# Moving one row in twenty-eight of the last weight matrix to 64 partitions, in a one-core decode block

## The chip, the cores and the metric

One core of a Trainium2 chip runs the kernel. The metric is the device time of one execution in microseconds (us): 139.9 us, the median of three executions (139.68 to 140.05).

## What is computed

A decode step of four sequences, one token each, through one transformer block: attention over the last 2048 positions of a cache (32 query heads, 4 key and value heads of 128 elements), and a gated feed-forward layer, each behind a layer norm and with a residual. Everything is bf16 in memory.

```python
def _B_ref(x, w1, w3, w2):                     # D = 1024, F = 3584
    gate = jnp.einsum("bsd,df->bsf", x, w1)
    up = jnp.einsum("bsd,df->bsf", x, w3)
    h = _silu(gate) * up
    out = jnp.einsum("bsf,fd->bsd", h, w2)
    return out
x = A_x
h = x + _A_ref(_layernorm(x, axis=-1), A_k_cache, A_v_cache, A_wq, A_wo)
h2 = h + _B_ref(_layernorm(h, axis=-1), B_w1, B_w3, B_w2)
```

With four tokens, nearly all of the work is to bring 55.6 MB of caches and weights into the core once.

## The kernel before, in words

**The stream.** All large inputs pass through a ring of five slots (`NSLOT`, 32 KB for each of 128 partitions). The list `ring` (L107 to L115) gives the order: keys, wq, values, wo, w1, w3, w2. `fill()` (L120 to L135) hands out the next slot as soon as the slot's former tenant is used, and issues the tenant's transfers from SyncE's queue at L133. A tenant is one transfer of up to 4 MB, or two of 2 MB (keys, values, and wo with `wo_` at L101), or, for the last slot of w2, three: `W2B = [16, 8, 2, 2]` (L108) cuts the 28 rows that each partition has of w2 into one slot of 16 rows and one slot of 8, 2 and 2. A partition's rows are adjacent in memory, `"(p fc) n -> p fc n"` (L79), and one row is 2 KB. In every one of these transfers each partition gets one piece, so one transfer is 128 pieces for the 16 DMA engines of the core.

**The order of the work** is the program's own order (`manual_schedule`). On SyncE's queue the transfers stand in the ring's order, and each waits for its slot. After attention, the output projection (L434, weights wo) gives h1 (L444); the second layer norm runs on VectorE (`layernorm_T`). `up_projection` (L448 to L466) is called for w1 and then for w3: for each of eight chunks of D, 8 matmuls (L458) of 448 columns fill two PSUM tiles of 32-partition groups. Between the two, ScalarE and VectorE make silu of the gate: exp (L472), plus one (L473), reciprocal (L474), multiply (L476). After w3, VectorE multiplies (L480) and transposes (L225) to `hg_T`, which has 28 groups of 128 values of F. The last matrix product (L491) takes w2's rows in the order in which their transfers come, four matmuls of 256 columns to a row, accumulating in one PSUM tile. VectorE adds h1 (L501), and two queues write the result (L503, L504).

**The two small transfers at the ends** matter for reading the trace. The input x is loaded by a transfer of ScalarE's queue (L149) whose access pattern has an outer dimension of 4 at its source and 16 partitions at its destination. Each half of the result is written by a transfer with an outer dimension of 2 at its destination.

Of the kernel before, what the change touches and what calls it, by code (L numbers as in the profile page):

```python
# [10 lines left out]
P = 128  # L11
ACT = mybir.ActivationFunctionType
ALU = mybir.AluOpType
AX = mybir.AxisListType
BF16 = mybir.dt.bfloat16
FP32 = mybir.dt.float32
# [7 lines left out]
def kernel(  # L24
# [20 lines left out]
    nc = tc.nc  # L45

    B, _, D = A_x.shape
    Hkv, Sk, Dh = A_k_cache.shape[1], A_k_cache.shape[2], A_k_cache.shape[3]
    NQ = A_wq.shape[1]
    Hq = NQ // Dh  # L50
    REP = Hq // Hkv
    W = min(4096, max(256, Sk // 4))
    F = B_w1.shape[1]
    KC = D // P
    FC = F // P
    NK = W // P
    C = 4
    R = 32
    S = R // B
    DQ = D // C  # L60
    FQ = F // C
    FH = FQ // 2
    assert B == C and Hkv == C and B * Hq == P and Dh == P and REP * Hkv == R
    assert D == KC * P and F == FC * P and W == NK * P and NQ == Hq * Dh
    eps = 1e-5
    qscale = float(Dh) ** -0.5

# [3 lines left out]
    T = REP  # L71
# [4 lines left out]
    wo_v = A_wo.rearrange("(g p t) n -> p g (t n)", g=Hkv, t=T)  # L76
    w1_v = B_w1.rearrange("(p kc) f -> p kc f", kc=KC)
    w3_v = B_w3.rearrange("(p kc) f -> p kc f", kc=KC)
    w2_v = B_w2.rearrange("(p fc) n -> p fc n", fc=FC)  # L79

    const = ctx.enter_context(tc.tile_pool(name="const", bufs=1))
    act = ctx.enter_context(tc.tile_pool(name="act", bufs=1))
# [3 lines left out]
    ps = ctx.enter_context(tc.tile_pool(name="ps", bufs=1, space=bass.MemoryType.PSUM))  # L86
# [6 lines left out]
    def pair(parts):  # L93
        return [parts[0:2], parts[2:4]]
# [3 lines left out]
        for name, cache in (("k", A_k_cache), ("v", A_v_cache))  # L98
    )
    kT_ = pair([("kT", b, [JR, P], None) for b in range(B)])  # L100
    wo_ = pair([("wo", g, [1, T * D], wo_v[:, g : g + 1, :]) for g in range(Hkv)])  # L101

    def four_rows(name, view, n):
        return [[(name, i, [4, n], view[:, 4 * i : 4 * i + 4, :])] for i in range(KC // 4)]

    wq_ = four_rows("wq", wq_v, NQ)
    ring = k_ + wq_[:1] + kT_ + wq_[1:] + v_ + wo_ + four_rows("w1", w1_v, F) + four_rows("w3", w3_v, F)  # L107
    W2B = [16, 8, 2, 2]  # L108
    w2_ = []
    f0 = 0  # L110
    for i, n in enumerate(W2B):
        w2_.append(("w2", i, [n, D], w2_v[:, f0 : f0 + n, :]))
        f0 += n
    ring += [w2_[:1], w2_[1:]]
    views = {}  # L115
    taken = []
    used = set()
# [1 line left out]
    def fill():  # L119

        while len(taken) < len(ring):
            n = len(taken) - NSLOT
            if n >= 0 and not all((name, i) in used for name, i, _, _ in ring[n]):
                break
            parts = ring[len(taken)]
            slot = stream.tile([P, SLOT], BF16, tag="slot", name="s_" + parts[0][0])
            o = 0
            for name, i, shape, src in parts:
                dst = slot[:, o : o + int(np.prod(shape))]
                o += int(np.prod(shape))  # L130
                view = dst.rearrange("p (a b) -> p a b", a=shape[0])
                if src is not None:
                    nc.sync.dma_start(out=dst if name in ("k", "v") else view, in_=src)  # L133
                views[(name, i)] = view
            taken.append(slot)  # L135

    def get(name, i):
        return views[(name, i)]

    def done(name, i):  # L140
        used.add((name, i))
        fill()
# [5 lines left out]
    nc.vector.memset(x_nat[:], 0.0)  # L148
    nc.scalar.dma_start(out=x_nat[::S, :], in_=x_flat.rearrange("b (c n) -> c b n", c=C))  # L149
    fill()  # L150

    ident = const.tile([P, P], BF16)
# [8 lines left out]
        out=t32[:], in_=ident[:].rearrange("p (q h) -> p h q", q=C), axis=AX.X, op=ALU.add  # L161
# [4 lines left out]
    for q in range(C):  # L166
# [3 lines left out]
        out=negm[:], in_=t32[:].rearrange("p (g r) -> p g r", g=Hkv), axis=AX.X, op=ALU.add  # L170
    )
    nc.vector.tensor_scalar(
        out=negm[:], in0=negm[:], scalar1=-1.0, scalar2=-NEG, op0=ALU.add, op1=ALU.mult
# [3 lines left out]
        out=jmask[:, :, 0], in_=ident[:].rearrange("p (j h) -> p j h", j=JM), axis=AX.X, op=ALU.add  # L177
# [6 lines left out]
    for l in range(2):  # L184
        nc.gpsimd.tensor_copy(
            out=strip[:, l, B - 1 :].rearrange("p (c x) -> p c x", c=C)[:, :, : B * Hkv].rearrange(
                "p c (g b) -> p c g b", b=B
            )[:, :, :, 0],
            in_=t32[:].rearrange("p (g c l) -> p l c g", g=Hkv, c=C)[:, l],
        )  # L190

    def layernorm_T(h_T, tag):

# [29 lines left out]
    def transpose_quads(dst, src, n):  # L223

        nc.vector.transpose(  # L225
            out=dst.rearrange("p j r -> p (j r)"), in_=src.rearrange("p (q j) -> p j q", j=n)
        )
# [24 lines left out]
    for i in range(KC // 4):  # L252
        w = get("wq", i)
        for kk in range(4):
            kc = 4 * i + kk
            for hf in range(2):
                for c in range(C):
                    o = (2 * c + hf) * HALF * Dh
                    nc.tensor.matmul(  # L259
                        q_ps[hf][R * c : R * c + R],  # L260
                        lhsT=xn_T[:, kc, :],
                        rhs=w[:, kk, o : o + HALF * Dh],
                        start=(kc == 0),
                        stop=(kc == KC - 1),
                        tile_position=(0, R * c),
# [12 lines left out]
    for b in range(B):  # L278
        nc.vector.tensor_copy(  # L279
            out=Qm[:, b].rearrange("p (g y) -> p g y", y=QW)[:, :, :REP],  # L280
            in_=qT_ps[:, :, :, S * b].rearrange("p r g -> p g r"),
# [125 lines left out]
    for l in range(2):  # L407
        for b in range(B):
            nc.tensor.matmul(  # L409
                on_ps[:, l],  # L410
                lhsT=strip[:, l, B - 1 - b : B - 1 - b + P],
                rhs=om[:, b],
                start=(b == 0),
                stop=(b == B - 1),
# [8 lines left out]
        out=oP[:, :, :, ::S],  # L423
        in_=oX[:, :, : Hkv * B].rearrange("p t (g b) -> p g t b", b=B),
# [2 lines left out]

    y_ps = ps.tile([P, DQ], FP32, tag="kt0")
    for g in range(Hkv):
        w = get("wo", g)  # L430
        for t in range(T):
            for c in range(C):
                o = t * D + c * DQ
                nc.tensor.matmul(  # L434
                    y_ps[R * c : R * c + R, :],
                    lhsT=oP[:, g, t, :],
                    rhs=w[:, 0, o : o + DQ],
                    start=(g == 0 and t == 0),
                    stop=(g == Hkv - 1 and t == T - 1),
                    tile_position=(0, R * c),  # L440
                )
        done("wo", g)
    h1 = act.tile([P, DQ], FP32)
    nc.vector.tensor_tensor(out=h1[:], in0=y_ps[:], in1=x_nat[:], op=ALU.add)  # L444
    h_T = act.tile([P, KC, R], FP32)
# [1 line left out]
    hn_T = layernorm_T(h_T[:], "ln2")  # L447


    def up_projection(name, out_ps):  # L450
        for i in range(KC // 4):
            w = get(name, i)
            for kk in range(4):
                kc = 4 * i + kk
                for hf in range(2):
                    for c in range(C):
                        o = c * FQ + hf * FH
                        nc.tensor.matmul(  # L458
                            out_ps[hf][R * c : R * c + R],
                            lhsT=hn_T[:, kc, :],  # L460
                            rhs=w[:, kk, o : o + FH],
                            start=(kc == 0),
                            stop=(kc == KC - 1),
                            tile_position=(0, R * c),
                        )
            done(name, i)  # L466

    gu_ps = [ps.tile([P, FH], FP32, tag=f"sc{i}", name=f"gu_ps{i}") for i in range(4)]
    up_projection("w1", gu_ps[:2])
    eg = act.tile([P, 2, FH], FP32)  # L470
    for hf in range(2):
        nc.scalar.activation(out=eg[:, hf], in_=gu_ps[hf][:], func=ACT.Exp, scale=-1.0)  # L472
    nc.vector.tensor_scalar_add(out=eg[:], in0=eg[:], scalar1=1.0)  # L473
    nc.vector.reciprocal(out=eg[:], in_=eg[:])  # L474
    for hf in range(2):
        nc.vector.tensor_tensor(out=eg[:, hf], in0=gu_ps[hf][:], in1=eg[:, hf], op=ALU.mult)  # L476
    up_projection("w3", gu_ps[2:])
    hg = act.tile([P, 2, FH], BF16)
    for hf in range(2):
        nc.vector.tensor_tensor(out=hg[:, hf], in0=gu_ps[2 + hf][:], in1=eg[:, hf], op=ALU.mult)  # L480
    hg_T = act.tile([P, FC, R], BF16)
    transpose_quads(hg_T[:], hg[:].rearrange("p a f -> p (a f)"), FC)


    y2_ps = ps.tile([P, DQ], FP32, tag="kt1")
    fc = 0
    for i, n in enumerate(W2B):
        w = get("w2", i)
        for ff in range(n):
            for c in range(C):  # L490
                nc.tensor.matmul(  # L491
                    y2_ps[R * c : R * c + R, :],
                    lhsT=hg_T[:, fc, :],
                    rhs=w[:, ff, c * DQ : (c + 1) * DQ],
                    start=(fc == 0),
                    stop=(fc == FC - 1),
                    tile_position=(0, R * c),
                )
            fc += 1
    res = act.tile([P, DQ], BF16)  # L500
    nc.vector.tensor_tensor(out=res[:], in0=y2_ps[:], in1=h1[:], op=ALU.add)  # L501
    out_v = out_flat.rearrange("b (c n) -> c b n", c=C)
# [32 lines left out]
```

## Time and profile before

| what | value |
|---|---|
| median of three executions | 139.9 us |
| the profiled execution | 140.13 us, span in the profile 138.3 us |
| busy: TensorE matmuls, VectorE, ScalarE, GpSimd | 80.2, 52.9, 42.7, 4.2 us |
| moved by SyncE's queue (q1) | 55.58 MB, 94.4% of 16 engines' span |
| mean rate over the span | 403 GB/s |
| last weights landed (trace, from the span's start) | 134.26 us |

The profile's times run from the first instruction to the last. A DMA queue's share is the time that its packets took, as a share of the span of all 16 DMA engines. Beside the page, the trace records when a transfer's semaphore was raised: each DMA engine that took part raises it once, when its own share has landed, so a transfer on 16 engines leaves 16 times. The waiting instruction goes on at the last of them.

### The profile page before, as it was taken

How to read it: one execution, taken by the hardware profiler on the slowest of the kernel's cores; microseconds unless marked ns; L12 is line 12 of the kernel's file. 1: busy time of each engine (PE TensorE's matmuls, PEld its weight loads, DVE VectorE, ACT ScalarE, POOL GpSimd, SP SyncE). 2: the span in 40 equal slices, each digit the busy share in tenths (PEclk: the TensorE clock that was granted, in tenths of full speed). 3: DMA queues.
4: the chain of work that ended last, by engine and by line, in shares of the span. 5: the costliest groups of instructions: out<-in, count | busy, mean ns of one | idle time of the engine just before them, and what ended most of it. 6: DMA issues, size and time to landing. Idle time of an engine off the chain costs nothing.

```text
span 138.3 us, 2012 instructions
## 1 busy us (share of the span) xinstructions
PE 80.2 (58%) x866; PEld 47.5 (34%) x868; DVE 52.9 (38%) x97; ACT 42.7 (31%) x57; POOL 4.2 (3%) x18
## 2 busy tenths in 40 slices
PE   0029898921903889328918998659539901703780
PEld 0029887820301322014304434537324400202550
DVE  3036676520000235177087197540330298350001
ACT  3005988850000325998807900000040200000000
POOL 7400000000000000000000000000000000000000
PEclk9999999998555799975797799965865896555555
DMA  4999999999989999999999999999999999999930
GB/s 152 399 423 431 431 436 455 455 441 398 445 384 426 441 417 417 450 407 431 450 400 431 433 469 431 394 448 448 419 398 448 456 411 430 445 407 398 406 148 2
DMA packets 3217, 55.72 MB, mean 403 GB/s; under 512 B 360, under 2 KB 392, under 8 KB 648
## 3 DMA queue, kind: packets, MB, share of 16 engines
q1 hardware_dynamic: 3178, 55.58, 94.4%
q8 instruction: 7, 0.11, 0.3%
q10 hardware_dynamic: 30, 0.01, 0.0%
q14 instruction: 2, 0.02, 0.0%
HBM read 55.58 MB, written 0.01 MB: 402 GB/s over the span
## 4 chain that ended last, share of the span: by engine, by line
DMA 49%; PE 27%; DVE 13%; ACT 4%; SPq 3%; issue 2%; DVEq 0%
DMA s_wq<-in_A_wq_dram 29%; DMA s_w<-in_B_w_dram 20%; PE o_ps L369 10%; PE y_ps L434 5%; ACT P L334 4%; PE sc_ps L294 3%; DVE PT L346 3%; SPq L133 3%; PE gu_ps L458 2%; PE q_ps L259 2%; DVE om L386 2%; DVE od L378 2%; PE on_ps L409 1%; PE tot_ps L355 1%; PE nm_ps L323 1%
## 5 line engine op out<-in xcount | busy, mean ns | idle before, releaser
L334 ACT ACTIVATE P<-sc_ps,bias 128x512 bf16<-128x512 f32 x16 | 19.7, 1417 | 9.6 <-DVE bias L331 9.6
L241 PE MATMUL kt_ps<-ident,s_k 128*128 128x128 bf16 x256 | 17.3, 228 | 1.3 <-ACT s_kT L245 1.0
L369 PE MATMUL o_ps<-s_v,PT 128*128 128x512 bf16 x62 | 17.5, 439 | 0.3 <-issue 0.2
L241 PEld LDWEIGHTS <-s_k 128*128 128x128 bf16 x256 | 16.3, 103 | 2.3 <-issue 1.7
L245 ACT COPY s_kT<-kt_ps 128x1024 bf16<-128x1024 bf16 x16 | 15.7, 1012 | 2.5 <-PE kt_ps L241 2.5
L458 PE MATMUL gu_ps<-s_w,n_T 128*32 128x448 bf16 x128 | 10.7, 513 | 8.8 <-DMA s_w<-in_B_w_dram 6.8
L259 PE MATMUL q_ps<-s_wq,n_T 128*32 128x512 bf16 x64 | 7.0, 615 | 11.8 <-DMA s_wq<-in_A_wq_dram 11.8
L243 DVE COPY s_kT<-kt_ps 128x1024 bf16<-128x1024 bf16 x16 | 11.1, 693 | 5.8 <-PE kt_ps L241 5.8
L491 PE MATMUL y_ps<-s_w,hg_T 128*32 128x256 bf16 x112 | 6.6, 418 | 8.0 <-DMA s_w<-in_B_w_dram 8.0
L369 PEld LDWEIGHTS <-PT 128*128 128x128 bf16 x64 | 7.2, 117 | 9.2 <-issue 4.4
L346 DVE STREAM_TRANSPOSE PT<-P 128x2048 bf16<-128x2048 bf16 x4 | 9.2, 2303 | 2.7 <-ACT P L334 2.7
L208 ACT ACTIVATE rstd<-rstd,eps_t 128x4 f32<-128x4 f32 x2 | 0.6, 297 | 29.5 <-DVE rstd L207 29.5
L458 PEld LDWEIGHTS <-n_T 128*32 128x32 bf16 x128 | 4.7, 131 | 14.1 <-issue 11.6
L294 PE MATMUL sc_ps<-s_kT,Qm 128*32 128x512 bf16 x64 | 8.5, 603 | 0.4 <-DVE Qm L279 0.4
L491 PEld LDWEIGHTS <-hg_T 128*32 128x32 bf16 x112 | 4.9, 142 | 10.0 <-issue 5.9
L259 PEld LDWEIGHTS <-n_T 128*32 128x32 bf16 x64 | 2.7, 137 | 15.6 <-issue 15.5
L269 DVE CAST q_sb<-q_ps 128x512 bf16<-128x512 f32 x1 | 0.7, 692 | 18.3 <-PE q_ps L259 18.3
L198 PE MATMUL sums_ps<-both,ones_f 128*128 128x64 f32 x4 | 1.1, 373 | 11.2 <-DVE both L196 11.2
L434 PE MATMUL y_ps<-s_wo,oP 128*32 128x256 bf16 x128 | 6.5, 397 | 1.7 <-DVE oP L422 1.7
L378 DVE SCALAR_TENSOR_TENSOR od<-o_ps,rinv,jmask 128x512 f32<-128x512 f32 x4 | 3.0, 751 | 8.4 <-PE o_ps L369 8.3
L270 ACT CAST q_sb<-q_ps 128x512 bf16<-128x512 f32 x1 | 0.6, 585 | 17.8 <-PE q_ps L259 17.8
L310 PE MATMUL mx_ps<-ident_f,rmax 128*1 128x128 f32 x8 | 1.7, 302 | 7.4 <-DVE rmax L308 7.4
(68 smaller groups left out, 64.7 us busy)
## 6 DMA issues: line engine op xcount, KB each, us to landing
s_w<-in_B_w_dram SPq DMA_DIRECT2D x4, 3584.0 KB, 21.2
s_k<-in_A_k_cache_dram SPq DMA_DIRECT2D x4, 2048.0 KB, 16.1
s_wq<-in_A_wq_dram SPq DMA_DIRECT2D x2, 4096.0 KB, 35.3
s_v<-in_A_v_cache_dram SPq DMA_DIRECT2D x4, 2048.0 KB, 25.1
s_wo<-in_A_wo_dram SPq DMA_DIRECT2D x4, 2048.0 KB, 25.5
s_w<-in_B_w_dram SPq DMA_DIRECT2D x1, 4096.0 KB, 28.0
s_w<-in_B_w_dram SPq DMA_DIRECT2D x1, 2048.0 KB, 25.7
s_w<-in_B_w_dram SPq DMA_DIRECT2D x2, 512.0 KB, 27.0
```

What stands on the lines that cost most here:

```text
L241: nc.tensor.transpose(out=kt_ps[:, jj], in_=k[:, jb * JB + jj, :], identity=ident[:])
L243: nc.vector.tensor_copy(out=kT[:, jb * JB : (jb + 1) * JB], in_=kt_ps[:])
L245: nc.scalar.copy(out=kT[:, jb * JB : (jb + 1) * JB], in_=kt_ps[:])
L259: nc.tensor.matmul(q_ps[hf][R * c : R * c + R], lhsT=xn_T[:, kc, :], rhs=w[:, kk, o : o + HALF * Dh], start=(kc == 0), stop=(kc == KC - 1) ...
L294: nc.tensor.matmul(sc_ps[b][R * q : R * q + R], lhsT=Qm[:, b, g * R : (g + 1) * R], rhs=v[:, g, q], start=(g == 0), stop=(g == Hkv - 1), t ...
L334: nc.scalar.activation(out=P4[:, :, :, g], in_=sc_ps[b][:].rearrange("p (j i) -> p j i", i=L5), func=ACT.Exp, bias=bias[:, g : g + 1], sca ...
L346: nc.vector.transpose(out=PT[:].rearrange("p j h -> p (j h)"), in_=stage.pop(("P4", b))[:].rearrange("p j i g -> p (j i g)"),)
L369: nc.tensor.matmul(o_ps[:], lhsT=PT[:, i * JM : (i + 1) * JM, :].rearrange("p j h -> p (j h)"), rhs=v[:, i * JM : (i + 1) * JM, :], start= ...
L378: nc.vector.scalar_tensor_tensor(out=od[:], in0=o_ps[:], scalar=rinv[:, 0:1], in1=jmask[:].to_broadcast([P, JM, Dh]), op0=ALU.mult, op1=AL ...
L434: nc.tensor.matmul(y_ps[R * c : R * c + R, :], lhsT=oP[:, g, t, :], rhs=w[:, 0, o : o + DQ], start=(g == 0 and t == 0), stop=(g == Hkv - 1 ...
L458: nc.tensor.matmul(out_ps[hf][R * c : R * c + R], lhsT=hn_T[:, kc, :], rhs=w[:, kk, o : o + FH], start=(kc == 0), stop=(kc == KC - 1), til ...
L491: nc.tensor.matmul(y2_ps[R * c : R * c + R, :], lhsT=hg_T[:, fc, :], rhs=w[:, ff, c * DQ : (c + 1) * DQ], start=(fc == 0), stop=(fc == FC ...
```

## The change

F = 3584 is 28 x 128. Before, every partition had 28 rows of w2. After, every partition has 27 (the first 3456 rows), and the remaining 128 rows go to the first 64 partitions, two for each. These two rows come in two transfers of 32 partitions (128 KB each), ahead of the slot's other three, and their source has an outer dimension of eight. The slot's first large transfer shrinks from 8 rows to 7.

The columns of w1 and w3 are divided accordingly: 3456 into halves of 432 columns for each of four groups, and 128 into two groups of 64 columns, which a third, small PSUM tile holds (tags kt2 and kt0). Each of the eight chunks of D so has two more matmuls, and exp, multiply and the last multiply have a third, small instruction each. A second, small transpose gives `hx_T`, and the last product has eight more matmuls (64 rows deep), which follow w2's first 16 rows; in place of the 28th row's four. Apart from this, the four transfers of wo become two of 4 MB in the same two slots. GpSimd clears a corner of `eg` once, early.

```diff
-    FC = F // P
+    FC = F // P - 1
+    FM = FC * P
+    XP = P // 2
+    XR = 2
...
-    FQ = F // C
+    FQ = FM // C
     FH = FQ // 2
+    FX = 32 * XR
...
-    w2_v = B_w2.rearrange("(p fc) n -> p fc n", fc=FC)
+    w2_v = B_w2[:FM].rearrange("(p fc) n -> p fc n", fc=FC)
+    w2x_v = B_w2[FM:].rearrange("(c i e y) n -> c e i (y n)", c=XP // R, i=4, e=8)
...
-    wo_ = pair([("wo", g, [1, T * D], wo_v[:, g : g + 1, :]) for g in range(Hkv)])
+    wo_ = [[("wo", i, [2, T * D], wo_v[:, 2 * i : 2 * i + 2, :])] for i in range(Hkv // 2)]
...
-    W2B = [16, 8, 2, 2]
+    W2B = [16, 7, 2, 2]
...
-    ring += [w2_[:1], w2_[1:]]
+    ring += [w2_[:1], [("w2x", 0, [XR, D], w2x_v)] + w2_[1:]]
...
-                if src is not None:
+                if name == "w2x":
+                    for c in range(XP // R):
+                        nc.sync.dma_start(out=dst[R * c : R * c + R], in_=src[c])
+                elif src is not None:
...
+    eg = act.tile([P, FQ + FX], FP32)
+    nc.gpsimd.memset(eg[XP:, FQ:], 0.0)
...
+                for c in range(XP // R):
+                    nc.tensor.matmul(
+                        out_ps[2][R * c : R * c + R],
+                        lhsT=hn_T[:, kc, :],
+                        rhs=w[:, kk, FM + c * FX : FM + (c + 1) * FX],
...
+    hx_T = act.tile([XP, XR, R], BF16)
+    nc.vector.transpose(
+        out=hx_T[:].rearrange("p y r -> p (y r)"),
+        in_=hg[:XP, FQ:].rearrange("p (i e y) -> p y e i", i=4, e=8),
+    )
...
+            down(hg_T[:, fc, :], w[:, ff], fc == 0, fc == FC - 1)
             fc += 1
+        if i == 0:
+            for y in range(XR):
+                down(hx_T[:, y, :], get("w2x", 0)[:XP, y], False, False)
```

`down` is the former four matmuls of a row in a function.

More of the change, by code (lines that the diff above doesn't have):

```diff
@@ L60 @@
     DQ = D // C
-    FQ = F // C
+    FQ = FM // C
     FH = FQ // 2
+    FX = 32 * XR
     assert B == C and Hkv == C and B * Hq == P and Dh == P and REP * Hkv == R
-    assert D == KC * P and F == FC * P and W == NK * P and NQ == Hq * Dh
+    assert D == KC * P and F == FM + XP * XR and W == NK * P and NQ == Hq * Dh
     eps = 1e-5
@@ L429 @@
     for g in range(Hkv):
-        w = get("wo", g)
+        w = get("wo", g // 2)
         for t in range(T):
@@ L436 @@
                     lhsT=oP[:, g, t, :],
-                    rhs=w[:, 0, o : o + DQ],
+                    rhs=w[:, g % 2, o : o + DQ],
                     start=(g == 0 and t == 0),
@@ L441 @@
                 )
-        done("wo", g)
+        if g % 2 == 1:
+            done("wo", g // 2)
     h1 = act.tile([P, DQ], FP32)
@@ L465, in up_projection @@
                         )
-            done(name, i)
[L468 to L472, printed above, removed]
+                for c in range(XP // R):
[3 more added lines that the diff above has]
+                        rhs=w[:, kk, FM + c * FX : FM + (c + 1) * FX],
+                        start=(kc == 0),
+                        stop=(kc == KC - 1),
+                        tile_position=(0, R * c),
+                    )
@@ new lines, in up_projection, with parts @@
+            done(name, i)
+    gate_ps, up_ps = (
+        [
+            ps.tile([P, n], FP32, tag=tag, name=f"{name}_{tag}")
+            for n, tag in zip((FH, FH, FX), tags)
+        ]
+        for name, tags in (("gate", ("sc0", "sc1", "kt2")), ("up", ("sc2", "sc3", "kt0")))
+    )
+    def parts(t, three):
+        yield t[:, :FH], three[0][:]
+        yield t[:, FH:FQ], three[1][:]
+        yield t[:XP, FQ:], three[2][:XP]
+    up_projection("w1", gate_ps)
+    for e, g in parts(eg, gate_ps):
+        nc.scalar.activation(out=e, in_=g, func=ACT.Exp, scale=-1.0)
@@ L473 @@
     nc.vector.tensor_scalar_add(out=eg[:], in0=eg[:], scalar1=1.0)
     nc.vector.reciprocal(out=eg[:], in_=eg[:])
[L475 to L480, printed above, removed]
-    hg_T = act.tile([P, FC, R], BF16)
-    transpose_quads(hg_T[:], hg[:].rearrange("p a f -> p (a f)"), FC)
@@ L485 @@
-    y2_ps = ps.tile([P, DQ], FP32, tag="kt1")
+    for e, g in parts(eg, gate_ps):
+        nc.vector.tensor_tensor(out=e, in0=g, in1=e, op=ALU.mult)
+    up_projection("w3", up_ps)
+    hg = act.tile([P, FQ + FX], BF16)
+    for (h, u), (e, _) in zip(parts(hg, up_ps), parts(eg, up_ps)):
+        nc.vector.tensor_tensor(out=h, in0=u, in1=e, op=ALU.mult)
+    hg_T = act.tile([P, FC, R], BF16)
+    transpose_quads(hg_T[:], hg[:, :FQ], FC)
+    hx_T = act.tile([XP, XR, R], BF16)
+    nc.vector.transpose(
+        out=hx_T[:].rearrange("p y r -> p (y r)"),
+        in_=hg[:XP, FQ:].rearrange("p (i e y) -> p y e i", i=4, e=8),
+    )
@@ L486, with down @@
+    y2_ps = ps.tile([P, DQ], FP32, tag="kt1")
+    def down(lhsT, rows, start, stop):
+        for c in range(C):
+            nc.tensor.matmul(
+                y2_ps[R * c : R * c + R, :],
+                lhsT=lhsT,
+                rhs=rows[:, c * DQ : (c + 1) * DQ],
+                start=start,
+                stop=stop,
+                tile_position=(0, R * c),
+            )
     fc = 0
@@ L489 @@
         for ff in range(n):
[L490 to L498, printed above, removed]
+            down(hg_T[:, fc, :], w[:, ff], fc == 0, fc == FC - 1)
             fc += 1
+        if i == 0:
+            for y in range(XR):
+                down(hx_T[:, y, :], get("w2x", 0)[:XP, y], False, False)
     res = act.tile([P, DQ], BF16)
```

## The prediction

> **What bounds the kernel now.** I read the DMA slices of the page first, then the end of the chain of waits, then the queues, and last the semaphore times of single DMA engines.
>
> ```profile
> DMA  4999999999989999999999999999999999999930
> GB/s 152 399 423 431 431 436 455 455 441 398 445 384 426 441 417 417 450 407 431 450 400 431 433 469 431 394 448 448 419 398 448 456 411 430 445 407 398 406 148 2
> ```
>
> The DMA engines are never idle between their first bytes and about 134 us. Compute stages come and go under this line without denting it.
>
> ```profile
> 106.04 0.33 SPq L133
> 106.37 0.05 issue
> 106.42 0.43 SPq L133
> 106.84 0.05 issue
> 106.89 27.36 DMA s_w<-in_B_w_dram
> 134.26 0.04 issue
> 134.30 0.64 PE y_ps L491 x8
> 134.97 0.42 DVE res L501
> ```
>
> The columns are start, duration and what. The last transfer is issued at 106.89 and lands at 134.26: it stands in a queue that is 27 us deep. What follows is a fixed tail, 138.3 - 134.26 = 4.0 us in the span. So the time is the landing of the last piece plus a constant, and the question is when each of the 16 engines is through with its bytes. The 16 semaphore times of the last transfer (2 rows for each partition, 32 KB for each engine), divided into two halves that the next paragraph tells apart:
>
> ```
> 132.24 132.34 132.38 132.40 132.44 132.46 132.46 133.06
> 132.75 133.52 134.04 134.14 134.15 134.17 134.17 134.26
> ```
>
> All engines have had the same number of bytes, yet they end 2.02 us apart, and everybody waits for the last. Where the lag comes from is told by comparing transfers. At the second key transfer the 16 engines already form two halves, eight at 12.71 to 12.87 and eight at 12.98 to 13.23. After that single engines jump back: at the fourth key transfer fifteen end by 23.01 and one at 24.30, so 1.3 us late.
>
> ```profile
> q8 instruction: 7, 0.11, 0.3%
> q14 instruction: 2, 0.02, 0.0%
> ```
>
> The packets of q8 are 16 KB each and start at 20.53, 29.70, 52.31, 87.44, 100.18, 112.94 and 133.48 us; after each of the first six, one more engine of the late half is about 1.3 us behind. That they are instruction code of TensorE fits its counts: it had started 295, 519, 730, 981, 1260, 1457 and 1724 instructions by then, steps of 197 to 279. The two of q14 (8 KB; 69.91 and 77.69 us) cost one engine of the late half 0.8 us and one of the early half 0.65. Followed from transfer to transfer, that gives the two rows above: seven undisturbed early engines, one early engine disturbed (133.06), one undisturbed late engine (132.75), one with the 8 KB loss (133.52) and the six with the 16 KB loss, which set the time.
>
> **Does the change move bytes off these engines?** The number of engines that a transfer uses is seen at the small ones: x, with an outer dimension of 4, raised its semaphore from four engines, and each half of the result, with an outer dimension of 2, from two. So an outer dimension of eight should use eight. Which eight: x's four packets of 5.59 to 5.71 us delay the engines that began a key packet at 4.971, 5.030, 5.044 and 5.058 us, and the eight early engines are those that began at 4.971 to 5.058, the late half at 5.163 to 5.477. The four that a small transfer takes all lie in the early half; I take it that the eight do, too. The Trainium skill (DMA: Bandwidth & Descriptors, Queues, rings and completion order) says that the lowest-numbered engines are used, as many as divide the outer dimensions, which agrees with the four and the two seen here.
>
> **The sum.** Every engine loses one row of eight partitions, 16 KB. The 8-row transfer (128 KB for each engine) landed last at 126.83 to 131.73, 4.90 us, so one row is 4.90 / 8 = 0.61 us. The eight engines of the two new transfers get 2 x 16 KB in 4 KB pieces; the last two transfers have the same pieces, and 32 KB took 134.26 - 132.97 = 1.29 on the last engine, 132.24 - 130.97 = 1.27 on the first. I take 1.27. So the early half ends 1.27 - 0.61 = 0.66 later and the late half 0.61 earlier. The six go to 133.43 to 133.65, the seven early ones to 132.90 to 133.12, the disturbed early engine to 133.72. The last is now 133.72: a gain of 134.26 - 133.72 = 0.54 us. The profiled execution goes from 140.13 to 139.59, and the median, 0.23 below it, to 139.36, which I write as 139.4.
>
> **What the rest of the change costs: nothing, under cover.** SyncE issues two transfers more at 106.04 (0.33 to 0.43 each by the rows above), so its last issue moves from 107.3 to some 108.2; the first bytes of that slot move at about 126, so 18 us cover it. The two wo issues that go away were 30 us ahead of need (landed 83.1, first used 92.3), and each pair shares a slot, so no slot comes free earlier or later.
>
> ```profile
> 109.62 0.63 DVE L473 TENSOR_SCALAR eg<-eg 128x896 f32<-128x896 f32 x1 [6.85 <-ACT eg L472]
> 110.28 5.75 DVE L474 RECIPROCAL eg<-eg 128x896 f32<-128x896 f32 x1
> 116.14 1.16 DVE L476 TENSOR_TENSOR eg<-gu_ps,eg 128x448 f32<-128x448 f32 x2
> 120.02 1.16 DVE L480 TENSOR_TENSOR hg<-gu_ps,eg 128x448 bf16<-128x448 f32 x2 [2.72 <-PE gu_ps L458]
> 121.21 1.70 DVE L225 STREAM_TRANSPOSE hg_T<-hg 128x896 bf16<-128x896 bf16 x1
> ```
>
> VectorE's rows grow from 896 to 928 columns: the reciprocal by 5.75 x 32/896 = 0.2. The small multiplies have no row of their own; they lie between 0.17 (the smallest operations of L204 to L211) and 0.58 (half of L476), and I take 0.25 by the 128x32 rows of 0.19 to 0.30. Of the small transpose the nearest row is the 128x256 one with 0.63. The gate so ends under 1.2 us later than 117.3, but is needed at 120.0 only, when w3's matmuls end. Those are 40 where 32 took 3.18, at most 0.8 more; multiplies and transposes are at most 1.2 more; `hg_T` is ready by 124.9 where it was at 122.9, and w2's first rows land at 126.8. Cover of 1.9 us; if that were gone, some 0.9 us more would hide, because TensorE is otherwise through with all earlier rows 0.9 us before the last piece lands (next).
>
> ```profile
> 126.88 3.61 PE L491 MATMUL y_ps<-s_w,hg_T 128*32 128x256 bf16 x64 [6.53 <-DMA s_w<-in_B_w_dram]
> 131.77 2.33 PE L491 MATMUL y_ps<-s_w,hg_T 128*32 128x256 bf16 x40 [1.28 <-DMA s_w<-in_B_w_dram]
> 134.30 0.62 PE L491 MATMUL y_ps<-s_w,hg_T 128*32 128x256 bf16 x8 [0.20 <-DMA s_w<-in_B_w_dram]
> ```
>
> TensorE's eight new matmuls, 8 x 0.056 = 0.45, end at 130.95; the 7-row piece lands at about 131.1, its 28 matmuls (40 took 2.33) end by 132.8, and the last eight wait for the landing at 133.72 as before. The tail is unchanged.
>
> **Rules against it.** The trace shows one engine 2.02 us behind another with equal bytes. The Trainium skill (same page, Rules for kernel authors) says to put a multiple of 16 outermost, so that all engines share, and not to split transfers by partition halves; by it, with equal engines, the added 0.66 would be pure loss. It counts engines and not their lag, so I go by the trace. The skill (Runtime: NRT & Kernel Launch, Instruction fetch mechanics) also calls the cost of a fetched block of 256 instructions mostly hidden; for the engine that fetches it this trace has 1.3 us.
>
> **The rivals.**
>
> *The seventh code fetch comes early.* The change adds 64 TensorE instructions before w2. The fetch that started at 133.48, behind the data, will start 72 instructions or so earlier in the program, which is between 130 and 133 us, with weights still to move. On the undisturbed late engine it costs nothing that shows (132.14 + 1.3 = 133.44). On the engine with the 8 KB loss it gives 132.91 + 1.3 = 134.21, on an early one up to 133.12 + 1.3 = 134.42: no change within 0.16, so 139.85 to 140.1. Its cost lies between 0.61 (its own bytes) and 1.3. For it: six fetches hit six different engines of the late half, and two are left. Against: it may start when these are done. 0.17.
>
> *Slower: that fetch meets an engine that was already hit.* From 133.65, 1.3 more is 134.95, a loss of 0.69: 140.6. It decides if the fetch starts before about 133 and the engines come round again before the two are used. Nothing before shows a second hit. 0.10.
>
> *The new transfers spread over 16 engines*, two partitions each. Then every engine has its old bytes, and the time is 139.9. The four and two seen speak against. 0.08. *They fall on the late half*: 134.26 + 0.66 = 134.92, so 140.6. x's engines speak against. 0.05.
>
> **How the numbers follow.** Forecast 0.60, from 139.1 (no early engine disturbed and the full 0.61, less a spread of 0.2) to 139.6. A measurement of this kernel can tell 0.3% (0.42 us) from no change, and the gain of 0.54 is barely over it: of the 0.60 I give 0.46 to faster and 0.14 to the same. The same in all is 0.14 + 0.17 + 0.08 = 0.39, slower 0.10 + 0.05 = 0.15. The range runs from 139.1 to 140.1 and leaves the two slower cases out.
>
> **What would show it.** Right: eight landings for each of the two new transfers, all of early engines; the last transfer's 16 times within about 1.0 us, the last at 133.6 to 133.8. Wrong: a seventh packet of q8 before 133 with an engine alone behind the others; or a wait of the last matmuls for anything but the DMA.

## The result, and the profile after

The changed kernel takes 140.21 us (median of 11, 140.07 to 140.40) against 139.97 us (median of 11, 139.57 to 140.11): a ratio of 1.0021, 95% interval 1.0012 to 1.0029. So it is slower by 0.2%, some 0.24 to 0.29 us, where a gain of 0.54 us had been forecast. The profiled execution took 140.18 us, with a span of 138.4 us.

The DMA slices of the changed kernel:

```profile
DMA  4999999999989999999999999999999999999930
GB/s 152 418 417 450 426 412 450 455 450 436 436 374 417 445 421 417 440 426 412 450 419 417 438 465 406 427 456 423 403 439 456 414 419 470 407 389 423 398 129 2
```

As before, the DMA engines are full to the end, at the same rate. The end of its chain of waits (start, duration, what):

```profile
106.04 0.83 SPq L141
106.87 0.06 issue
106.92 0.72 SPq L141
107.65 0.04 issue
107.69 0.43 SPq L143
108.12 0.04 issue
108.16 0.43 SPq L143
108.59 0.04 issue
108.64 25.80 DMA s_w2x<-in_B_w_dram
134.43 0.04 issue
134.47 0.64 PE y_ps L529 x7
135.12 0.02 issue
135.14 0.42 DVE res L548
```

The shape is the same: the last transfer's landing, then a fixed tail. The landing is at 134.43, where it was at 134.26. The two new issues (L141) cost SyncE 0.83 and 0.72 us, more than the 0.33 to 0.43 of the other issues, and delay nothing: the transfer waits 25.80 us in its queue. TensorE's last product:

```profile
126.64 3.61 PE L529 MATMUL y_ps<-s_w,hg_T 128*32 128x256 bf16 x64 [6.46 <-DMA s_w<-in_B_w_dram]
130.18 0.61 PE L529 MATMUL y_ps<-s_w2x,hx_T 64*32 64x256 bf16 x8
131.97 2.11 PE L529 MATMUL y_ps<-s_w2x,hg_T 128*32 128x256 bf16 x36 [1.18 <-DMA s_w2x<-in_B_w_dram]
134.47 0.62 PE L529 MATMUL y_ps<-s_w2x,hg_T 128*32 128x256 bf16 x8 [0.40 <-DMA s_w2x<-in_B_w_dram]
```

In the brackets stands the idle time and what ended it: before each group after the eight new matmuls TensorE waits for the DMA and nothing else. So the loss must lie in when single DMA engines end. The semaphore times of the second new transfer and of the last transfer of w2:

```
126.04 126.05 126.06 126.09 126.15 126.80 127.05 127.63
131.75 131.76 132.00 132.86 132.86 132.87 132.97 133.25 133.27 133.28 133.36 133.37 133.60 133.85 134.42 134.43
```

The new transfer did land from eight engines. But they are not eight early ones: five are together, two are behind by 0.7 and 1.0 us (as engines with an 8 KB code fetch were before), and one by 1.5 us, like an engine with a 16 KB code fetch. It can be followed through the next transfers, 131.93, 133.18, 134.42: it is one of the two engines that the kernel waits for, and the other (134.43) is taken up below. The engines that got nothing are through by 133.37.

### The profile page after: what moved, and what is told of

The parts are those of the page before. It is cut to its first block, busy times and chain, and to the rows that moved or that the text cites. A ratio compares the mean times of both kernels' runs of the same rounds, so it can differ in the third digit from the quotient of the medians.

```text
span 138.4 us, 2092 instructions
## 1 busy us (share of the span) xinstructions
PE 80.8 (58%) x904; PEld 49.7 (36%) x904; DVE 53.3 (39%) x100; ACT 42.8 (31%) x58; POOL 4.4 (3%) x19
## 4 chain that ended last, share of the span: by engine, by line
DMA 47%; PE 28%; DVE 13%; SPq 4%; ACT 4%; issue 2%; DVEq 0%
DMA s_wq<-in_A_wq_dram 29%; DMA s_w2x<-in_B_w_dram 19%; PE o_ps L382 10%; PE y_ps L447 5%; ACT P L347 4%; PE sc_ps L307 3%; DVE PT L359 3%; SPq L143 3%; PE gate_sc L472 2%; PE q_ps L272 2%; DVE om L399 2%; DVE od L391 2%; SPq L141 1%; PE on_ps L422 1%; PE tot_ps L368 1%
## 5 line engine op out<-in xcount | busy, mean ns | idle before, releaser
L472 PEld LDWEIGHTS <-n_T 128*32 128x32 bf16 x128 | 5.6, 128 | 11.0 <-issue 7.8
L472 PE MATMUL up_sc<-s_w,n_T 128*32 128x432 bf16 x64 | 5.1, 453 | 6.6 <-DMA s_w<-in_B_w_dram 6.6
L272 PEld LDWEIGHTS <-n_T 128*32 128x32 bf16 x64 | 2.6, 137 | 15.6 <-issue 15.4
L529 PE MATMUL y_ps<-s_w,hg_T 128*32 128x256 bf16 x64 | 3.6, 419 | 6.5 <-DMA s_w<-in_B_w_dram 6.5
L472 PE MATMUL gate_sc<-s_w,n_T 128*32 128x432 bf16 x64 | 6.0, 546 | 1.9 <-DVE n_T L231 1.9
```

What stands on the lines that cost most here:

```text
L272: nc.tensor.matmul(q_ps[hf][R * c : R * c + R], lhsT=xn_T[:, kc, :], rhs=w[:, kk, o : o + HALF * Dh], start=(kc == 0), stop=(kc == KC - 1) ...
L472: nc.tensor.matmul(out_ps[hf][R * c : R * c + R], lhsT=hn_T[:, kc, :], rhs=w[:, kk, o : o + FH], start=(kc == 0), stop=(kc == KC - 1), til ...
L529: nc.tensor.matmul(y2_ps[R * c : R * c + R, :], lhsT=lhsT, rhs=rows[:, c * DQ : (c + 1) * DQ], start=start, stop=stop, tile_position=(0, R ...
```

## The experiments

**Who are the eight?** Two kernels, before and after, with five tiny transfers behind the last weights, of outer dimension 2, 4, 6, 8 and 12.

```diff
+            if len(taken) == len(ring):
+                for n, k in enumerate((2, 4, 6, 8, 12)):
+                    m = 256 + 32 * n
+                    nc.sync.dma_start(out=slot[:k, 14000 + 400 * n : 14000 + 400 * n + m], in_=B_w2[:k, :m])
```

> The kernel before with five tiny transfers (outer dimension 2, 4, 6, 8 and 12; 0.5 to 0.8 KB for each engine) at the end of SyncE's queue, behind the last weights. Each raises its semaphore from so many engines, each time behind that engine's own weights, so the nested sets tell which engines are late. Prediction's theory: the set of eight lies in the early half, all under 133.2 us, and all engines hit by a 16 KB code fetch are outside of it. Rival (the after trace hints at it): at least one of the eight is an engine hit by a 16 KB fetch, so one of the eight lands at about 133.7 to 134.2.

One execution: 140.09 us. The semaphore times of the last weights, and below them those of the tiny transfers with outer dimension 2, 4, 6 and 8:

```
132.36 132.37 132.38 132.40 132.46 132.53 132.54 132.72 133.38 133.48 133.86 134.01 134.08 134.10 134.15 134.19
k=2: 132.72 133.55
k=4: 132.63 132.90 133.66 133.72
k=6: 132.56 132.81 133.07 133.84 133.90 134.06
k=8: 132.58 132.59 132.74 132.98 133.25 134.01 134.06 134.26
```

As many landings as the outer dimension, each time. The sets are nested, and each further tiny transfer on an engine lands 0.16 to 0.20 us later (133.55, 133.72, 133.90 on one), so the new members can be told. Call an engine tight that no code fetch has put back, and 8 KB or 16 KB loss what a fetch of that size costs its engine. The first two engines are a tight one and one with an 8 KB loss, the next two the same, the third pair a tight one and one at 134.06, which has the full 16 KB loss, the fourth pair two tight ones. So the rival expectation holds: the eight hold one of the six engines with a 16 KB loss, and both engines with the smaller loss; the other five of the six lie outside.

> The changed kernel with the same five tiny transfers behind the last weights. Theory T (one engine among the eight of the new transfers had a 16 KB code fetch, and 0.66 us more on it sets the end): of the eight, one or two land at 134.3 to 134.5, the other six at 132.8 to 133.9; the eight others end by 133.4 except for none. Rival U (the seventh code fetch, now earlier, alone sets the end): the engine that is last is one that no earlier fetch had hit, and only it is beyond 134.

One execution: 140.44 us. The tiny transfer of outer dimension 6 ended at 134.69 on its last engine, the one of 4 at 134.30 and of 2 at 134.08: again the engine that comes in with the third pair is last. The last weights landed at 133.91, 134.12 and 134.50, the five engines with a 16 KB loss that lie outside at 133.49 to 133.71. Here one engine alone sets the end, as theory T has it. The other engines were later than it had them: 134.12 among the eight, where it allowed 133.9, and 133.71 outside, where it allowed 133.4. The size fits: in the probe of before this engine had its weights at 133.86 (one step of 0.20 before 134.06), and the forecast's own 0.66 more gives 134.52, against 134.50 here.

**Transfers or instructions?** Four kernels. The instructions of the change with the old transfers of w2 (the matmuls on the new rows read others):

```diff
-    w2_v = B_w2[:FM].rearrange("(p fc) n -> p fc n", fc=FC)
+    w2_v = B_w2.rearrange("(p fc) n -> p fc n", fc=FC + 1)
...
+        n += i == 1
...
-    ring += [w2_[:1], [("w2x", 0, [XR, D], w2x_v)] + w2_[1:]]
+    ring += [w2_[:1], w2_[1:]]
...
-                down(hx_T[:, y, :], get("w2x", 0)[:XP, y], False, False)
+                down(hx_T[:, y, :], w[:XP, y], False, False)
```

> The changed kernel's instructions with the transfers of w2 as before (28 rows for every partition in pieces of 16, 8, 2 and 2; no new transfers). The eight matmuls that would read the two new rows read two rows of the first piece again, so that part of the last product is computed from other rows of w2 than the reference has. The merged wo stays. Theory T (the 0.66 us more on eight engines, one of which had a 16 KB code fetch, is the cost): the last landing goes back by 0.2 to 0.35 us and the time to that of before (140.0, within 0.15). Rivals U and V (the earlier code fetch, the added instructions, the merged wo): it stays 0.2 to 0.3 us above before.

This kernel (m1): 139.93 us against 139.93, ratio 0.9996 (0.9984 to 1.0007). The cost is gone, though all added instructions on TensorE, VectorE and ScalarE and the merged wo are still there. This also shows that these cost nothing that can be measured. (The two added issues are gone too, with their transfers.)

The reverse, the old instructions with the new transfers:

```diff
+    w2_v = B_w2[: 27 * P].rearrange("(p fc) n -> p fc n", fc=27)
+    w2x_v = B_w2[27 * P :].rearrange("(c i e y) n -> c e i (y n)", c=2, i=4, e=8)
...
-    W2B = [16, 8, 2, 2]
+    W2B = [16, 7, 2, 2]
...
+    ring += [w2_[:1], [("w2x", 0, [2, D], w2x_v)] + w2_[1:]]
```

> The kernel before, its instructions kept, with the changed kernel's transfers of w2 alone (27 rows, and the two transfers on 64 partitions with outer dimension eight). The 28th row of the last product is read from 64 partitions of the new transfers, half as deep, so that row's part of the output is computed from half of the values. Theory T: slower by 0.2 to 0.3 us, as the change; one engine of the eight lands last, alone, near 134.5. Rivals U and V: no difference from before (within 0.1).

This kernel (m2): 140.44 against 139.93, 1.0032 (1.0022 to 1.0043). The new transfers alone, with their two issues, make the loss. The last transfer's end is 133.68, 134.01 and, alone, 134.71; the fetch that the old code makes late started at 133.74 here, too late for it. The loss, some 0.45 to 0.51 us, is larger than theory T had it (0.2 to 0.3) and than that of the change. The profile shows why it can be: here the late engine among the eight was the last of its six when w2's first rows had landed (126.65 of 126.46 to 126.65; it is the one at 127.29 after the first new transfer), so nothing of the 0.66 us was hidden, and in the changed kernel it was the first of its six (126.38 of 126.38 to 126.60).

The old transfers with the added matmuls of the up projections alone (32 matmuls of 64 columns each, into PSUM tiles that nobody reads):

```diff
+                for c in range(2):
+                    nc.tensor.matmul(
+                        more[R * c : R * c + R],
+                        lhsT=hn_T[:, kc, :],
+                        rhs=w[:, kk, 64 * c : 64 * c + 64],
```

> The kernel before with the 32 additional matmuls of 64 columns in the two up projections, into PSUM tiles that nobody reads; transfers as before. Theory T: the seventh code fetch starts earlier than 133.48, on an engine that has time (132.3 + 1.3 = 133.6), so no change, 139.97 within 0.15. Rival U: the fetch hits an engine that is already late, or the added instructions cost by themselves: 140.2 or more.

This kernel (d1): 140.13 against 140.03, 1.0001 (0.9992 to 1.0010). The seventh code fetch did move, from 133.48 to 131.97, and met an engine that had time: nothing is at 134 but the engines that were there before. In the changed kernel it starts at 132.24, and the engine at 134.43 beside the one at 134.42 is probably its doing (one of the five tight ones is missing in the last row). If so, the fetch alone would have set the same end in that execution. The loss does not need it, since the probe of after and the kernel with the new transfers alone have one engine alone at the end, at 134.50 and 134.71.

And twice the dose:

```diff
-    FC = F // P - 1
+    FC = F // P - 2
...
-    XR = 2
+    XR = 4
...
-    W2B = [16, 7, 2, 2]
+    W2B = [16, 6, 2, 2]
```

> The changed kernel with 26 rows for every partition and four more, in place of two, for the first 64 (8 KB pieces), so that the same eight engines get twice the extra. Theory T: 0.6 to 0.7 us more on the engine that is last: 140.8 to 141.0, the last landing at 135.0 to 135.2, with all eight others through by 133. Rivals U and V: as the change, 140.2 within 0.2, because the number of instructions hardly differs.

140.91 (four executions) against 139.93: 1.0065 (1.0048 to 1.0082), within the bounds of theory T. The last landing is at 135.06, 0.63 after that of the change, within its bounds too. Of the eight engines outside, four end by 131.35 and four at 133.40 to 133.65, where theory T had them through by 133; the eight loaded ones end at 132.61 to 135.06.

**Is it eight engines at all that matters?** The new transfers with an outer dimension of 32, so that all 16 engines take part:

```diff
-    w2x_v = B_w2[FM:].rearrange("(c i e y) n -> c e i (y n)", c=XP // R, i=4, e=8)
+    w2x_v = B_w2[FM:].rearrange("(c p y) n -> c p (y n)", c=XP // R, p=R)
...
-        in_=hg[:XP, FQ:].rearrange("p (i e y) -> p y e i", i=4, e=8),
+        in_=hg[:XP, FQ:].rearrange("p (q y) -> p y q", y=XR),
```

> The changed kernel with the two new transfers spread over 16 engines (32 pieces, one for each partition, outer dimension 32 in place of eight, rows given to partitions in plain order); all instructions, sizes and issues stay. Theory T (bytes on eight engines): every engine has its old bytes, the last landing goes back to about 134.1 to 134.3 and the time to that of before, 139.97 within 0.15. Rival V (what the change costs is in the added issues or instructions): it stays at 140.2. Rival U (the earlier code fetch): it stays at 140.1 to 140.3 if the fetch meets a late engine, 139.9 to 140.0 if it meets an early one.

This kernel (s1): 142.07 (four executions) against 140.03, 1.0145 (1.0124 to 1.0165). None of the theories had that; equal bytes should have brought the old time back. Its DMA slices:

```profile
DMA  4999999999999999999999999999999999999940
GB/s 149 412 415 438 429 433 470 391 433 447 447 415 396 438 433 429 405 443 433 436 401 440 453 424 420 457 416 432 453 408 408 440 455 447 401 295 232 399 169 2
```

The engines stay busy, but two slices, around 123 to 130 us, move 295 and 232 GB/s in place of some 400. There the two new transfers pass, and with them the transfer ahead of them, whose last rows came at 128.36 in place of 126.6. So I tried the same two transfers, on 16 engines too, to partitions that lie spread over all 128 (the matmuls read other rows):

```diff
-                        nc.sync.dma_start(out=dst[R * c : R * c + R], in_=src[c])
+                        nc.sync.dma_start(out=dst[2 * c :: 4], in_=src[c])
```

> As the spread over 16 engines that came out at 142.1, but the two new transfers write partitions 0, 4, 8, ... 124 and 2, 6, ... 126 in place of 0 to 31 and 32 to 63; the eight matmuls read rows of the first piece in their place, so that part of the last product is computed from other rows. Theory W (in the slow spread, engines wrote to partitions that other engines were writing too, and 256 KB went to the side of SBUF that serves 64 partitions): evenly over the partitions, the time falls to 140.0 to 140.7. Rival X (a transfer with 32 pieces of 4 KB on 16 engines is slow by itself): it stays at 142.0.

This kernel (q1): 140.13 against 139.93, 1.0012 (1.0001 to 1.0024). Its slices at the same place:

```profile
GB/s 142 390 437 441 427 427 465 455 422 427 427 389 432 432 408 441 432 408 450 427 405 450 420 479 407 411 432 473 407 403 440 473 403 439 446 390 405 395 171 2
```

The dip is gone (390 and 405), and each of the two transfers passes in some 0.31 us on every engine (124.91, 125.22, 125.54 on the first; 124.88, 125.61, 126.23 in the slow spread). So it is not the small pieces that are slow but where they go. The Trainium skill (SBUF — State Buffer, Door 1: The DMA port swizzle) says that a partition's number decides which of 16 ports its bytes come in by, and that partitions 0 to 63 reach eight of them. The two runs agree with that, with 2 us between them. Eight engines into the same 64 partitions, as in the change, are not slow: 16 KB take an engine 0.63 us there (125.41 to 126.04), close to the 0.61 us of 16 KB in the 8-row transfer. So it is the 16 engines and the 64 partitions together; which engines get in each other's way, and why it makes as much as 2 us, no run shows.

**Is it code that makes an engine late?** The kernel before, with the tiny transfers and 128 more small matmuls while TensorE waits for wq:

```diff
+        for _ in range(64):
+            nc.tensor.matmul(extra_ps[:R], lhsT=xn_T[:, 0, :], rhs=ident[:, :64], start=True, stop=True)
         w = get("wq", i)
```

> The kernel before, with the five tiny transfers at the end of the queue, and with 128 additional small matmuls (64 columns, with a weight load each, into PSUM that nobody reads) while TensorE waits for wq, so that 256 more instructions are fetched. If a code fetch is what puts a DMA engine back by 1.3 us: eight packets of 16 KB in q8, seven of them before 130 us, and seven engines in place of six some 1.4 to 1.9 us behind the tight ones at the last transfer, the last landing within 0.15 of before (134.2) where the added fetch meets a fresh engine, and 1.3 us later (135.5) where it meets one a second time. If the lag has another cause (a property of those engines, contention), six engines lag as before.

This kernel (f1): 139.98 against 140.02, 0.9999 (0.9989 to 1.0009). From its queues:

```profile
q8 instruction: 8, 0.13, 0.4%
q14 instruction: 2, 0.02, 0.0%
```

Eight packets, at 21.19, 29.56, 38.13, 53.36, 89.00, 101.79, 114.76 and 132.75 us. The last transfer but one ends on its engines at 130.85 to 131.39 (seven), 131.66, 131.94, and then at 132.48, 132.53, 132.67, 132.71, 132.74, 132.81 and 132.86: seven engines behind, where it had been six. One more fetch, one more late engine, and no more time, since the others were late already.

## Why the prediction was wrong

- **What bounds the kernel** was right: the last engine's last bytes plus a constant tail. In every profiled execution without tiny transfers the time is 5.66 to 5.99 us above the last landing. So the tail is constant to 0.3 us, and a loss of 0.2 us is told by medians of many executions and not by two single profiles.
- **Lag from code fetches** was right (f1), and so was the number of engines that an outer dimension gives.
- **The step that failed** is "The four that a small transfer takes all lie in the early half; I take it that the eight do, too", and with it that the six late engines all lose bytes. The probes show one of the six among the eight, in the third pair, which x's four engines do not reach. The two engines with the smaller loss lie among the eight, too, one in each of the first two pairs, so among four such as x uses; the prediction had put one of these two in the late half. The trace of before shows that x's four were already misread. The engine that began a key packet at 5.030 us was held up by x's packets (5.710, 6.341, 6.971 and 7.760 us) and by a key packet of 0.77 us (at 6.995, where most took 0.61). It closed the first key transfer with a packet at 7.783 us; the eight early engines closed it at 7.407 to 7.658. So one of the four was in the late half when the second key transfer, from which the halves were read, began. Followed packet by packet, it is the engine that the 8 KB fetch at 69.91 us hit.
- **The terms of the sum** were of the right size. The new transfers took 126.04 - 124.77 = 1.27 us on the first engine (1.27 forecast), and the row that went away gave 4.90 - (130.76 - 126.46) = 0.60 on a late engine outside (0.61). Laid on the right engine, they give 133.86 + 0.66 = 134.52, and 134.50 was measured. The rival on the other side (they fall on the late half, 134.92, 140.6) had the right sign and mechanism, but five of the six were outside, and the sixth was the least late in the changed kernel's profile and in the probe of before: 0.2 to 0.3 us of the 0.66 were hidden by the others.
- **The earlier seventh fetch** came as described (132.24), and an engine at 134.43 fits the 134.42 that this rival gave for an early engine. But the loss does not need it (m1 with it, at 131.93: no loss; m2 without it: the loss). Its cost was put between 0.61 and 1.3 us; it was some 1.5 us in the changed kernel's profile, if that engine is its doing, and no more than some 0.3 us on any engine in d1 and m1. Why it differs so stays open.
- **Nothing under cover** was right for the instructions and wo (m1, 0.9996). The two issues cost SyncE 0.83 and 0.72 us, twice what was put down for them, but the transfer behind them then waits 25.80 us; the kernel q1, which has both issues, bounds what they can cost at 0.24% (1.0001 to 1.0024).
- **The rival of a spread over 16 engines**, two partitions each, was put at the old time and would have been wrong by 2 us (s1): I had counted bytes for each engine and not where they are written.

## What to carry to other kernels

Where a kernel is bound by its DMA to the end, as this one, its time is that of the slowest of 16 engines, and moving bytes between engines pays only if it is known engine by engine who is late: nested tiny transfers behind the last one tell that in one profile. A subset of the engines is no evidence for a larger one, and an order read at the start of a trace must be followed to the end before it is used there. For a small transfer, try the destination partitions as well as the number of engines: at equal bytes for each engine, they made the 2 us between s1 and q1.

## What had not been expected

- A transfer of 2 x 128 KB on 16 engines into 64 neighbouring partitions cost 2 us (142.07 against 140.03); into partitions spread over all 128 it cost some 0.1% (140.13 against 139.93; interval 0.0 to 0.2%).
- In the stream, a code fetch of 16 KB put its DMA engine back by 1.3 us, about twice the 0.61 us of its bytes, and successive fetches met different engines: six of them, then seven, all late by a similar amount. The seventh fetch of the other kernels, near the end, did not follow that (0.3 us or less in two of them).
- Which engines are hit is not quite fixed: of the eight, one had a 16 KB loss in the changed kernel, in both probes and with the new transfers alone, two in the kernel with the double dose.
